# Four linear-attention and gated feed-forward layers on one core: the last segment by halves, keys of odd heads by DMA, the map of q by pairs

## The chip, the core and the metric

The kernel runs on one core of a Trainium2 chip. Its engines run side by side, each in the order of its own instructions: TensorE (PE in the profile, with its weight loads as PEld), VectorE (DVE), ScalarE (ACT), GpSimd (POOL) and SyncE (SP), which here only issues DMAs. The metric is the time of one execution on the device in microseconds; the median of several runs counts.

## The reference

The input x has 2048 rows of 512. Four blocks follow one another, each on a layer norm and added to x: attention, feed-forward, attention, feed-forward, both attention blocks with the same weights and both feed-forward blocks too.

```python
for s in range(4):                                    # segments of 512 rows; 32 heads of 16
    logits = einsum('bhqd,bhkd->bhqk', qs, ks) * scale + causal_mask
    a_dot  = einsum('bhqk,bhkd->bhqd', softmax(logits), vs)
    pq     = phi(qs)                                  # phi(t) = t + 1 where t > 0, else exp(t)
    a_mem  = einsum('bhld,bhde->bhle', pq, M) / (einsum('bhld,bhd->bhl', pq, z)[..., None] + 1e-6)
    out_s  = g * a_mem + (1 - g) * a_dot              # g = sigmoid(beta) of each head
    M, z   = M + phi(ks)^T vs, z + sum(phi(ks))
x = x + concat(out) @ wo
x = x + (gelu(norm(x) @ w_gate) * (norm(x) @ w_up)) @ w_down     # inner width 1792
```

## The kernel before

The work is cut into eight passes k = 0 to 7: segments 0 to 3 of the first pair of blocks, then of the second. A pass has an attention part (class `Att`) and a feed-forward part (class `Ffn`). All weights and x stay in SBUF. Passes overlap: while the feed-forward products of one pass run, TensorE also does the scores of the next and the q, k and v of one after that.

The order of all instructions is made in Python before anything is built. `Clocks` and `Engine` keep a book of when each engine would be free, with a cost for each kind of instruction. Work for TensorE that needs a PSUM bank is an `Item` with a due time (`DUE`, `DUE_STEP`, `BIAS`, in passes) and a condition; the main loop (L1150) takes score steps as they become possible, else the ready item that is due first, else a half score step, else a product of ones that only fills (L1181). `Engine.post` puts work on the other engines with a slack: the lower it is, the sooner the work is taken. SP takes DMAs in the order that the book gives, and an engine waits in order: what stands behind a waiting instruction waits too.

Dense work goes through `product` (L406): four matmuls of 128 rows by 32 columns of weights, one in each column group, with up to 512 moving columns. Gate, up, down, q, k, v, wo, the update of M and the memory term all use it, so they share line 411. Scores (L805) use row groups instead, so that the array changes its tiling between a score step and dense work.

In a pass, `scores` does 20 steps, five for each two blocks of four even and four odd heads (a block b is 128 of the 512 columns of q). A step fills two PSUM tiles st of 128x1024, one for each pair of heads, which ACT's exponential (L834) turns into pt; GpSimd's affine_select (L825) then zeroes what lies above the diagonal. A step may be issued in two halves, one st tile at a time. `flush_item` multiplies pt by the values (L853), for the even and then the odd heads of a block; DVE transposes (byq, L865), takes the reciprocal of the row sums (L869), scales (ab, L873), transposes back (aT, L880) and adds the memory term amT (L883). When aT has its four blocks, `wo` adds to x (L920), `Norm` takes row statistics (L434, L442) and GpSimd the inverse deviation rs (L452), DVE scales rows to xn (L464), and xn is turned into xnT by a DMA transpose (`turn_later`, L376) or, for the feed-forward norms of passes 0, 1 and 7, by products with an identity matrix. Then come 14 gate products of four steps each with the gelu on ACT (L943), 14 up products with a multiplication on DVE (L990), and for each of four row tiles a down product of 14 steps.

In a group of 32 rows the even head's keys are the first 16, which the scores read alone from kf; for the odd heads they read all 32 rows of a copy kB in which the even head's rows are zero: `k_done` makes it for each block by a multiplication with maskB (L562), on DVE in pass 0 and on GpSimd later. `phi` makes the feature map of one block of q or k: ACT's exp into one of three e tiles (L619), DVE's min with 1 (L637), and max(x, 0) + e (L623); that of k is then turned by a DMA transpose into phik.

The vaug tiles hold the values with a column for the denominators; DVE writes these columns and the constants of the gate in `gate_constants` and `later_constants` (L348 to L368).

Of the kernel before, what the change touches and what calls it, by code (L numbers as in the profile page):

```python
# [19 lines left out]
H = 32  # L20
# [15 lines left out]
PAIRS = 5  # L36
STEPS = 4 * PAIRS
# [3 lines left out]
SETS = 3  # L41
HALF_FROM = 0
# [4 lines left out]
QK_DUE = 0.628  # L47
E_Q = -0.224
E_K = 0.898

FLUSH_WAIT = 3.455
PIECE_SLACK = 1.942
URGENT, SOON, NORMAL = -5.367, -1.509, 0.0
EXP_SLACK, E_SLACK, PHI_SLACK, GELU_SLACK = -0.824, 4.309, 2.973, 1.704
ACT_EVICT, FIRST_EVICT = 1.257, 1.549
XN_BUFS = 3
KB_DVE = 1
KB_SLACK = 4.7
HALF_STEPS = 1
MARGIN = 1.0  # L60
MEM_SLACK = 0.593


DUE = {"wo": 0.876, "gate": 1.264, "up": 1.3, "down": 1.912, "upd": 0.119, "mem": 0.057, "v": -0.028}
DUE_STEP = {"gate": 0.0055, "up": 0.02, "down": 0.0585}
BIAS = {
    **{("qk", k): d for k, d in {2: 0.223, 3: 0.042, 4: 0.068, 5: 0.154, 6: 0.166, 7: 0.076}.items()},
    **{("mem", k): d for k, d in {1: -0.292, 4: -0.311, 5: 0.04, 6: -0.044, 7: -0.105}.items()},
    **{("down", k): d for k, d in {0: 0.059, 1: -0.073, 4: -0.059, 5: 0.029, 6: 0.023, 7: -0.054}.items()},
    **{("upd", k): d for k, d in {0: -0.005, 1: 0.321, 2: -0.019, 3: 0.19}.items()},  # L70
    **{("v", k): d for k, d in {0: 0.085, 2: -0.091, 3: -0.008, 4: -0.177, 5: -0.177, 6: 0.177}.items()},
    **{("wo", k): d for k, d in {1: 0.024, 2: -0.93, 3: -0.666, 4: 0.027, 5: -0.086, 7: -0.094}.items()},
    **{("gate", k): d for k, d in {1: -0.2, 3: -0.043, 4: -0.093, 5: 0.014}.items()},
    **{("up", k): d for k, d in {0: 0.121, 2: -0.039, 4: -0.056, 5: -0.013, 6: 0.024}.items()},
}

# [52 lines left out]
class Clocks:  # L129
# [4 lines left out]
    SWITCH = 0.097  # L134
# [56 lines left out]
    def has(self, *names, by=None):  # L191
        t = self.pe if by is None else by
        return all(self.ev.get(n, 1e9) <= t for n in names)


class Slots:


    def __init__(self, ck, n):
        self.ck, self.free, self.queue = ck, list(range(n)), []  # L200

    def take(self, fn):
        self.queue.append(fn)
        self.turn()

    def turn(self):
        while self.free and self.queue:
            self.queue.pop(0)(self.free.pop(0))
# [28 lines left out]
def kernel(  # L237
# [52 lines left out]
    pieces = [(14.0, 512, lambda: load_x(2)), (27.0, 512, lambda: load_x(3))]  # L290
    for kt in range(KT):
        pieces.append((32.0 + 1.2 * kt, 128, lambda kt=kt: load(w_att["o"][:, kt, :], w_view(A_wo)[:, kt, :])))
    for n, (sb, w) in enumerate(((wg_sb, B_w_gate), (wu_sb, B_w_up))):
        for kt in range(KT):
            for h in range(2):
                c = slice(FF * h // 2, FF * (h + 1) // 2)
                pieces.append((37.0 + 1.6 * (8 * n + 2 * kt + h), 224, lambda sb=sb, w=w, kt=kt, c=c: load(
                    sb[:, kt, c], w_view(w)[:, kt, c])))
    for h in range(7):
        r = slice(2 * h, 2 * h + 2)  # L300
        pieces.append((94.0 + 2.0 * h, 256, lambda r=r: load(
            wd_sb[:, r, :], B_w_down.rearrange("(ft p) n -> p ft n", p=P)[:, r, :])))

# [37 lines left out]
    zacc = cst.tile([P, 4], F32, name="zacc")  # L341
    vaugs = [cst.tile([P, TPS, VW + 15], BF16, name=f"vaug{i}") for i in range(SETS)]

# [4 lines left out]
    def gate_constants():  # L348
        nc.vector.tensor_scalar(out=cden[:], in0=tmp_e[:], scalar1=1.0, scalar2=None, op0=ALU.add)
        nc.vector.tensor_scalar(out=tmp_e2[:], in0=tmp_e2[:], scalar1=1.0, scalar2=None, op0=ALU.add)  # L350
        nc.vector.reciprocal(out=tmp_e2[:], in_=tmp_e2[:])


    def later_constants():
        def column(va):
            nc.vector.tensor_copy(out=by_head(va)[:, :, :, DH], in_=cden[:].unsqueeze(1).to_broadcast([P, TPS, H]))
            nc.vector.memset(va[:, :, VW:], 0.0)
# [7 lines left out]
        for n, va in enumerate(vaugs):  # L365
            ck.dve.post(13.0 + 3.0 * n, NORMAL, (0.4, lambda va=va: column(va), None))
        for b in range(4):
            ck.dve.post(20.0 + b, NORMAL, (0.28, lambda b=b: scale(b), None))  # L368
# [50 lines left out]
    xn_slots = Slots(ck, XN_BUFS)  # L419

    class Norm:
        def __init__(self, key, tt0, tag, slack, free):
            self.key, self.tt0, self.tag, self.slack, self.free = key, tt0, tag, slack, free
            self.mv, self.n, self.left = None, 0, TPS
# [4 lines left out]
        def stats(self, j, ready):  # L429
# [6 lines left out]
            def told(t):  # L436
                self.n += 1
                if self.n == TPS:
                    self.scales(t)
# [4 lines left out]
        def scales(self, ready):  # L444
            def first():
                self.ve = wrk.tile([P, TPS, 1], F32, tag="lnve", name="ve")
                nc.gpsimd.tensor_scalar(out=self.ve[:], in0=self.mv[:, :, 1:2], scalar1=EPS_LN, scalar2=None,
                                        op0=ALU.add)

            def second():  # L450
                self.rs = self.small("rs", 1)
                nc.gpsimd.tensor_tensor(out=self.rs[:], in0=self.ve[:], in1=mhalf[:], op=ALU.pow)  # L452

            ck.pool.post(ready, URGENT, (0.25, first, None),
                         (1.05, second, lambda t: ck.when(self.free, lambda: self.start(max(t, ck.pe)))))

        def start(self, ready):
            self.xnT = seg.tile([P, KT, L], BF16, tag=self.tag, bufs=1, name="xnT")
            for j in range(TPS):
                xn_slots.take(lambda i, j=j: self.row(j, i, max(ready, ck.pe)))  # L460
# [7 lines left out]
        def row(self, j, i, ready):  # L468
            xn = Box(lambda: self.normed(j, i))

            def landed(t):
                xn_slots.back(i, t)
                self.left -= 1
                if not self.left:
                    ev[self.key] = t

            def told(t):
                if self.key in BY_PE:
                    items.append(self.turn_item(j, xn, t, landed))
# [4 lines left out]
            ck.dve.post(ready, self.slack, (0.46, xn, told))  # L484
# [25 lines left out]
    items = []  # L510
    e_jobs = []
    e_slots = Slots(ck, 3)
# [3 lines left out]
    class Att:  # L516
        def __init__(self, k):
# [3 lines left out]
            self.ab, self.aT, self.amT, self.n_qkv, self.n_am, self.n_num = {}, None, {}, 0, 0, 0  # L521
# [7 lines left out]
        def add_items(self):  # L529
# [5 lines left out]
            def first():  # L535
                self.q, self.kf, self.kB = (seg.tile([P, KT, L], BF16, tag=f"{n}{k % SETS}", bufs=1, name=n)
                                            for n in ("q", "kf", "kB"))
# [11 lines left out]
            def q_done(b, ps):  # L549
                def told(t):  # L550
                    ev["q", k, b] = t
                    if s > 0:
                        e_jobs.append((k - E_Q + 0.03 * b, t, lambda: k < 2 or ("memn", k - (1 if s > 1 else 2)) in ev,
                                       lambda r, sl: self.phi(b, "q", r, sl)))

                evict(ps, lambda: self.q[:, b, :], lambda: ps()[:], told)

            def k_done(b, ps, at=None):
                def told(t):
                    ev["k", k, b] = t  # L560
                    eng, job, cost = (nc.vector, ck.dve, 0.345) if k < KB_DVE else (nc.gpsimd, ck.pool, 1.566)
                    job.post(t, KB_SLACK if k else NORMAL, (cost, lambda: eng.tensor_scalar(  # L562
# [654 lines left out]
```

## Time and profile before

| | us |
|---|---|
| median of 3 runs (lowest to highest) | 558.88 (557.92 to 559.39) |
| the profiled execution | 559.25 |
| its span, first to last instruction | 557.5 |
| first score step, last score step | 12.2, 496.5 |
| score exponentials on ACT (320) | 309.9 |
| masks on POOL (448) | 202.6 |
| granted clock of TensorE | 1.000 |

The span is what the trace covers; the rest of the profiled execution lies around it. Many numbers of the profile are busy times of an engine; busy on TensorE includes matmuls that run one over another, so how often products start says more than how long each took. A line such as "PE L411 MATMUL m<-xnT,wg_sb 128*32 128x512 bf16" names the engine, the line of the code, the operation, what is written and read, the shape of the weights and the moving columns.

### The profile page before, as it was taken

The page shows a single profiled execution, that of the slowest core. Times are in us where ns is not written, and L with a number is a line of the kernel's source. Part 1 is how long each engine was busy: PE and PEld are TensorE (multiplying, and loading weights), DVE is VectorE, ACT ScalarE, POOL GpSimd, SP SyncE. Part 2 cuts the span into 40 slices and gives each one's busy share as a digit, 9 for nine tenths or more (in the row PEclk, how much of TensorE's full clock was granted, in tenths as well). Part 3 has the DMA queues.
Part 4 walks back from the last instruction along what each step waited for, and adds up shares of the span by engine and source line. Part 5 has one row for each costly group of instructions (what it writes and reads, how often), then busy time and mean ns, then how long its engine had stood idle before and what let it go on. Part 6 is the DMA issues. An engine that isn't in the chain of part 4 may idle for free.

```text
span 557.5 us, 24388 instructions
## 1 busy us (share of the span) xinstructions
PE 547.4 (98%) x10882; PEld 255.0 (46%) x10882; DVE 436.5 (78%) x838; ACT 446.8 (80%) x553; POOL 270.4 (48%) x520
## 2 busy tenths in 40 slices
PE   8999999999999999999999999999989999999997
PEld 3333445444544444444444445444444444445554
DVE  5987996999969996788948899689856897577061
ACT  3999999987999789997898979989788877860600
POOL 2688973365814465274725656148522764130000
PEclk9999999999999999999999999999999999999999
DMA  7236611510041033110310033100530005000001
GB/s 226 43 95 219 125 21 32 144 42 2 16 75 31 4 40 68 21 31 4 60 21 12 3 57 56 37 12 5 96 50 3 2 9 101 12 2 31 12 2 40
DMA packets 64361, 25.96 MB, mean 47 GB/s; under 512 B 54272, under 2 KB 64256, under 8 KB 64256
## 3 DMA queue, kind: packets, MB, share of 16 engines
q1 hardware_dynamic: 64112, 24.40, 20.6%
q8 instruction: 85, 1.39, 1.0%
q14 instruction: 20, 0.16, 0.1%
q10 hardware_dynamic: 144, 0.01, 0.0%
HBM read 9.71 MB, written 2.10 MB: 21 GB/s over the span
## 4 chain that ended last, share of the span: by engine, by line
PE 83%; DVE 10%; ACT 2%; DMA 1%; issue 1%; POOL 1%; SPq 0%; ACTq 0%
PE m L411 68%; PE st L805 9%; PE m L853 6%; ACT pt L834 1%; DVE x_sb L920 1%; DVE byq L865 1%; DVE xn L464 1%; DVE e L623 1%; DVE gel L990 1%; ACT gel L943 1%; DMA phik<-e 1%; DVE e L637 1%; DVE phiq L623 1%; DMA x_sb<-in_A_x_dram 1%; DVE aT L880 1%
## 5 line engine op out<-in xcount | busy, mean ns | idle before, releaser
L834 ACT ACTIVATE pt<-st 128x1024 bf16<-128x1024 f32 x320 | 309.9, 1027 | 48.7 <-PE st L805 44.3
L825 POOL TENSOR_SCALAR_AFFINE_SELECT pt<-pt 128x256 bf16<-128x256 bf16 (+1 forms) x448 | 202.6, 471 | 218.0 <-ACT pt L834 212.4
L990 DVE TENSOR_TENSOR gel<-gel,m 128x512 bf16<-128x512 bf16 x112 | 75.3, 684 | 44.2 <-PE m L411 34.8
L411 PE MATMUL m<-xnT,wg_sb 128*32 128x512 bf16 x1792 | 106.6, 380 | 0.7 <-ACT xnT L403 0.7
L411 PE MATMUL m<-wd_sb,gel 128*32 128x512 bf16 x1792 | 106.8, 380 | 0.1
L411 PE MATMUL m<-xnT,wu_sb 128*32 128x512 bf16 x1792 | 105.8, 380 | 0.1
L411 PEld LDWEIGHTS <-wu_sb 128*32 128x32 bf16 x1792 | 46.5, 97 | 45.5 <-issue 5.7
L411 PEld LDWEIGHTS <-wg_sb 128*32 128x32 bf16 x1792 | 46.0, 97 | 44.8 <-issue 7.4
L411 PEld LDWEIGHTS <-gel 128*32 128x32 bf16 x1792 | 45.5, 97 | 45.3 <-issue 7.2
L920 DVE TENSOR_TENSOR x_sb<-x_sb,m 128x512 bf16<-128x512 bf16 x64 | 42.3, 673 | 17.4 <-PE m L411 17.4
L865 DVE STREAM_TRANSPOSE byq<-m 128x512 f32<-128x512 f32 x64 | 45.3, 707 | 12.6 <-PE m L853 12.6
L853 PE MATMUL m<-pt,vaug 128*32 128x512 bf16 (+3 forms) x1024 | 46.2, 300 | 0.6 <-DVE gel L990 0.5
L562 POOL TENSOR_SCALAR kB<-kf,maskB 128x512 bf16<-128x512 bf16 x28 | 45.0, 1608 | 1.8 <-DVE kf L402 1.1
L805 PE MATMUL st<-q,kB 32*128 32x384 bf16 (+3 forms) x512 | 39.6, 300 | 1.3 <-ACT pt L834 1.3
L434 DVE BATCH_NORM_STATS2 st<-x_sb 128x6 f32<-128x512 bf16 x60 | 40.5, 675 | 0.1
L805 PE MATMUL st<-q,kf 16*128 16x384 bf16 (+3 forms) x512 | 40.1, 302 | 0.1
L943 ACT ACTIVATE gel<-m 128x512 bf16<-128x512 f32 x63 | 34.8, 602 | 3.7 <-PE m L411 3.5
L853 PEld LDWEIGHTS <-vaug 128*32 128x32 bf16 x1024 | 26.0, 97 | 23.0 <-issue 2.1
L411 PE MATMUL m<-xnT,wk_sb 128*32 128x512 bf16 x496 | 35.4, 381 | 0.0
L411 PE MATMUL m<-xnT,wq_sb 128*32 128x512 bf16 x496 | 34.0, 380 | 0.0
L411 PE MATMUL m<-wv_sb,xnT 128*32 128x512 bf16 x512 | 33.9, 380 | 0.0
L805 PEld LDWEIGHTS <-kf 16*128 16x128 bf16 x512 | 11.9, 91 | 43.7 <-issue 42.2
(92 smaller groups left out, 568.5 us busy)
## 6 DMA issues: line engine op xcount, KB each, us to landing
out_dram<-x_sb SPq DMA_DIRECT2D x16, 128.0 KB, 1.8
wg_sb<-in_B_w_gate_dram SPq DMA_DIRECT2D x8, 224.0 KB, 4.4
wu_sb<-in_B_w_up_dram SPq DMA_DIRECT2D x8, 224.0 KB, 4.6
wd_sb<-in_B_w_down_dram SPq DMA_DIRECT2D x7, 256.0 KB, 4.2
x_sb<-in_A_x_dram SPq DMA_DIRECT2D x3, 512.0 KB, 6.7
xnT<-xn SPq DMA_TRANSPOSE x48, 2.5
x_sb<-in_A_x_dram SPq DMA_DIRECT2D x4, 128.0 KB, 3.1
wv_sb<-in_A_wv_dram SPq DMA_DIRECT2D x1, 512.0 KB, 7.6
```

Source lines behind the costliest of these rows:

```text
L411: nc.tensor.matmul(out[r], lhsT=lhsT[:, r], rhs=rhs, start=start, stop=stop, tile_position=(0, 32 * c))
L434: nc.vector.bn_stats(out=self.st6[:, 0, :], in_=x_sb[:, self.tt0 + j, :])
L562: job.post(t, KB_SLACK if k else NORMAL, (cost, lambda: eng.tensor_scalar(out=self.kB[:, b, :], in0=self.kf[:, b, :], scalar1=maskB[:, 0:1 ...
L623: nc.vector.scalar_tensor_tensor(out=dst, in0=src, scalar=0.0, in1=e[0][:], op0=ALU.max, op1=ALU.add, accum_out=self.zk[:, b:b + 1] if whi ...
L805: nc.tensor.matmul(sts[j // 2][:, j % 2, c0:c0 + N], lhsT=lhsT[rows, b, P * ki:P * ki + P], rhs=self.q[rows, b, P * ki:L], start=True, sto ...
L825: nc.gpsimd.affine_select(out=dv, in_=dv, pattern=[[0, w], [1, P]], compare_op=ALU.is_ge, fill=0.0, base=0, channel_multiplier=-1)
L834: ck.act.post(max(begun + 0.4, self.step_from), EXP_SLACK, (1.024, lambda st=st, pt=pt: nc.scalar.activation(out=pt[:], in_=st[:], func=AC ...
L853: nc.tensor.matmul(ps()[32 * j:32 * j + 32, P * ki:L], lhsT=self.vaug[:, ki, h * (DH + 1):h * (DH + 1) + 32], rhs=two[j // 2][:, j % 2, c0 ...
L865: nc.vector.transpose(out=self.byq[:, par, :, :].rearrange("p a c -> p (a c)"), in_=ps()[:])
L920: ck.dve.post(ck.made(), slack, (0.683, lambda: nc.vector.tensor_tensor(out=xt, in0=xt, in1=ps()[:], op=ALU.add), lambda t: (ps.read(t), t ...
L943: return lambda: nc.scalar.activation(out=out(), in_=in_(), func=ACT.Gelu_apprx_tanh)
L990: ck.dve.post(ck.made(), NORMAL, (0.683, lambda: nc.vector.tensor_tensor(out=g, in0=g, in1=ps()[:], op=ALU.mult), lambda t: (ps.read(t), e ...
```

## The change

Five things are done:

1. Pass 7, the last segment, is cut into two halves of 256 rows. `steps_of` gives its 20 score steps anew: first the six that the first half of the queries needs, then 14 for the second. A flush then covers even and odd heads of a block for one half, so that there are still eight. Norm, gate, up and down run for each half; gate and up products have 256 moving columns, and two of the 14 inner tiles share a PSUM bank.
2. kB lies in three fixed tiles. Those of index 1 and 2 are set to zero by GpSimd at the start; from pass 1 on, the odd heads' rows come by four DMAs on SP, of 16 partitions and 4 KB in each, when all four blocks of the keys are there. Pass 0 still multiplies on DVE.
3. The map of q is made for two blocks at once and in the phiq tile itself, without e tiles; e has two tiles now, for k alone.
4. The vaug columns are made on GpSimd ahead of the first products, and the gate's constants on DVE from 45 us of the plan on.
5. The order is planned anew: other due times, slacks and margins (1.7 us more for the transposes of phi of k, 1.5 for kB), four xn buffers, one of them kept for feed-forward rows and for pass 1, the back-transposition of a chunk no longer waiting for amT, and gate products that start the gelu part waiting for an earlier one's hold. The book's clock is set to 12.1 us after the opening part (10.9 before). The weights' DMAs keep their times.

```diff
-FLUSH_WAIT = 3.455
-URGENT, SOON, NORMAL = -5.367, -1.509, 0.0
-EXP_SLACK, E_SLACK, PHI_SLACK, GELU_SLACK = -0.824, 4.309, 2.973, 1.704
-XN_BUFS = 3
+FLUSH_WAIT = 4.904
+URGENT, SOON, NORMAL = -11.142, -0.462, 0.0
+EXP_SLACK, E_SLACK, PHI_SLACK, GELU_SLACK = -0.745, 5.402, 3.22, 1.514
+XN_BUFS = 4
+XN_KEPT = 1
+E_BUFS = 2
+PHI_MARGIN = 1.7
+KB_MARGIN = 1.5
...
+SPLIT = {NK - 1}
+def steps_of(k):
...
+    for b in (0, 2):
+        wide = [[(c, par, 0, 0, HALF, HALF * par) for par in range(2)] for c in (b, b + 1)]
+        narrow = [(c, par, 1, P, HALF, P * (2 * (c - b) + par)) for c in (b, b + 1) for par in range(2)]
+        found += [(wide[0], []), (narrow, [(b, None, 0)]), (wide[1], [(b + 1, None, 0)])]
...
+    kBs = [cst.tile([P, KT, L], BF16, name=f"kB{i}") for i in range(SETS)]
+    for kB in kBs[1:]:
+        nc.gpsimd.memset(kB[:], 0.0)
...
+    def value_constants():
+        nc.gpsimd.tensor_scalar(out=cden[:], in0=tmp_e[:], scalar1=1.0, scalar2=None, op0=ALU.add)
+        for va in vaugs:
+            nc.gpsimd.tensor_copy(out=by_head(va)[:, :, :, DH], in_=cden[:].unsqueeze(1).to_broadcast([P, TPS, H]))
+            nc.gpsimd.memset(va[:, :, VW:], 0.0)
...
+                for g in range(4):
+                    r = slice(32 * g + 16, 32 * g + 32)
+                    ck.sp.post(t, KB_SLACK, (0.55, lambda r=r: nc.sync.dma_start(
+                        out=self.kB[r], in_=self.kf[r]), lambda t2: ck.at(t2 + 1.8, lambda: landed(t2 + 2.0))))
...
-                    eng, job, cost = (nc.vector, ck.dve, 0.345) if k < KB_DVE else (nc.gpsimd, ck.pool, 1.566)
-                    job.post(t, KB_SLACK if k else NORMAL, (cost, lambda: eng.tensor_scalar(
+                    if k == 0:
+                        ck.dve.post(t, NORMAL, (0.5, lambda: nc.vector.tensor_scalar(
...
+        def phi_q(self, half, ready, slack):
+            two = slice(2 * half, 2 * half + 2)
...
+                nc.scalar.activation(out=self.phiq[:, two, :], in_=self.q[:, two, :], func=ACT.Exp)
...
+                nc.vector.tensor_scalar(out=self.phiq[:, two, :], in0=self.phiq[:, two, :], scalar1=1.0, scalar2=None,
+                                        op0=ALU.min)
...
+                nc.vector.scalar_tensor_tensor(out=self.phiq[:, two, :], in0=self.q[:, two, :], scalar=0.0,
+                                               in1=self.phiq[:, two, :], op0=ALU.max, op1=ALU.add)
...
+            def grown(w, ps, g, h):
+                return [(Clocks.MM[512] / self.parts + 0.0012 * (self.parts - 1),
+                         lambda kt=kt, f=f, n=n: product(ps()[:, n * L // self.parts:(n + 1) * L // self.parts],
+                                                         w[:, kt, f * P:(f + 1) * P], self.norm.xnT[:, kt, cols(h)],
+                                                         kt == 0, kt == KT - 1))
+                        for n, f in enumerate(tiles(g)) for kt in range(KT)]
```

554 lines of the change are left out of this document (324 added, 230 removed).

## The prediction

> **What bounds the kernel now.** I read the page first, then busy time by stage, then the chain of waits, then the timelines of the three places where TensorE is not simply working.
>
> ```profile
> PE 547.4 (98%) x10882; PEld 255.0 (46%) x10882; DVE 436.5 (78%) x838; ACT 446.8 (80%) x553; POOL 270.4 (48%) x520
> PE 83%; DVE 10%; ACT 2%; DMA 1%; issue 1%; POOL 1%; SPq 0%; ACTq 0%
> ```
>
> TensorE carries 83% of the chain. Busy is not useful, though, so I cut the span at the places where its work changes:
>
> ```profile
> 0.00:12.20 12.20, 10.21 (x54) 4.78 (x55) 5.90 (x19) 3.70 (x7) 3.53 (x14) 1.00 0.81 249
> 12.20:66.40 54.20, 54.20 (x905) 20.79 (x908) 47.63 (x103) 53.22 (x66) 43.05 (x77) 1.00 0.45 116
> 66.40:80.10 13.70, 13.57 (x328) 6.41 (x328) 13.07 (x30) 13.58 (x18) 10.83 (x19) 1.00 0.34 60
> 80.10:125.00 44.90, 43.03 (x936) 20.85 (x932) 37.91 (x72) 41.78 (x55) 21.57 (x38) 1.00 0.28 67
> 125.00:404.00 279.00, 278.73 (x5724) 128.76 (x5716) 235.18 (x454) 245.10 (x299) 147.53 (x287) 1.00 0.18 32
> 404.00:409.00 5.00, 3.29 (x108) 1.83 (x100) 2.05 (x5) 2.49 (x5) 1.79 (x4) 1.00 0.61 88
> 409.00:496.60 87.60, 87.60 (x1765) 40.49 (x1762) 66.56 (x114) 74.02 (x88) 39.28 (x78) 1.00 0.13 24
> 496.60:554.30 57.70, 56.81 (x1104) 31.04 (x1096) 27.59 (x49) 12.94 (x20) 2.79 (x6) 1.00 0.06 19
> ```
>
> The columns are window, length, then busy us of PE, weight loads, DVE, ACT, POOL, the clock and the DMA share. From 12 to 80 us ACT is full (53.22 of 54.20, 13.58 of 13.70); TensorE is "busy" but pads:
>
> ```profile
> L411 PE MATMUL m<-warm 128*32 128x512 bf16 x44 | 3.5, 383 | 0.0
> 63.53 2.56 PE L411 MATMUL m<-wo_sb,aT 128*32 128x512 bf16 x44
> 66.02 0.39 PE L805 MATMUL st<-q,kB 32*128 32x512 bf16 x4
> 66.34 0.40 PE L411 MATMUL m<-wo_sb,aT 128*32 128x512 bf16 x4
> 517.78 36.47 PE m L411 x672
> 12.20:66.40 54.20, 14.62 (x152) 4.05 (x152) 1.00 0.45 116
> 125.00:404.00 279.00, 38.62 (x584) 11.00 (x584) 1.00 0.18 32
> ```
>
> The last dense stretch prices a product (four matmuls): 36.47/672 x 4 = 0.217 us; the 44 filler matmuls are 11 products, 2.4 us. A score stretch costs its own 0.32 (66.02 to 66.34) plus 0.10 that the dense stretch before it runs over (44 x 0.0543 = 2.39, but 2.49 from start to start): 0.42. A step done in two halves pays that twice. The two windows of score matmuls alone hold 152 and 584; at 6.4 a step that is 24 and 91 steps, which the PE timeline shows in 37 and 96 stretches; 66 to 80 us has 8 for 5, 80 to 125 us 14 for 13. So 16 extra stretches before 80.1 (6.7 us), one to 125, five after (2.1 us).
>
> **The change, stage by stage.**
>
> *Before the first gate product (12.2 to 80.1).* Padding here is 6.7 + 2.4 = 9.1 us. It exists because dense work is missing until the first feed-forward block may start, 13.7 us after its last wo product (66.34; the first gate product is at 80.09):
>
> ```profile
> 66.47 2.94 ACT pt L834 x3
> 69.47 1.78 POOL pt L825 x4
> 71.70 1.51 POOL rs L452
> 73.23 1.22 DVE xn L464 x3
> 76.11 0.69 DVE xnT L402
> 78.65 0.68 DVE xnT L402
> L562 POOL TENSOR_SCALAR kB<-kf,maskB 128x512 bf16<-128x512 bf16 x28 | 45.0, 1608 | 1.8 <-DVE kf L402 1.1 <-ACT kf L403 0.6
> L619 ACT ACTIVATE e<-q 128x512 bf16<-128x512 bf16 x24 | 15.4, 644 | 1.1 <-DVE ab L873 1.1
> L943 ACT ACTIVATE gel<-gel 128x1024 bf16<-128x1024 bf16 x21 | 22.4, 1068 | 0.0
> L623 DVE SCALAR_TENSOR_TENSOR phiq<-q,e 128x512 bf16<-128x512 bf16 x24 | 18.0, 749 | 0.8
> ```
>
> These are rs, xn and its turn, waiting their turn behind masks, feature maps and evictions. The change takes 28 x 1.608 = 45 us off POOL; makes the exponentials of q 12 x 1.068 = 12.8 instead of 15.4 us of ACT; makes the adds 12 pieces between 0.749 (all fixed) and 1.498 us (none fixed), so 9 to 18 against 18.0 us of DVE (I take 15.5); moves the vaug columns from DVE to POOL; and keeps one xn buffer for feed-forward rows with more urgency. None of these engines ends the chain for long, so their savings count only here. The rows of the chain itself sum to 8.8 us of the 13.7; some 5 are queueing. I take 4 us of the 9.1; bounds 0 (exponentials still fill ACT) and 9.1.
>
> *80.1 to 125.* Idle 44.90 - 43.03 = 1.9 plus one stretch, 2.3 in all, where TensorE waits on masks, gelus and the chunk transposes. Lighter DVE and POOL should take half: -1.2, bounds 0 and -2.3.
>
> *125 to 496.6.* There TensorE has 279.00 - 278.73 = 0.3 idle, five stretches (2.1) and one stall of 5.00 - 3.29 = 1.7, while a transpose lands:
>
> ```profile
> 402.22 3.93 DMA phik<-e
> DMA to landing us min/median/max: 2.4/2.5/4.6
> ```
>
> It landed 1.4 us beyond its median. The new plan books 1.7 us more for these transposes (PHI_MARGIN), about what was lost. -1.7 of 4.1, bounds 0 and -4.1. What is late next if the transpose slips again is the update of M, then the mem products; dense work stands ahead of them in the new order.
>
> *The tail.* After the last score at 496.6 all is dense. Only 57.70 - 56.81 = 0.9 is idle, mostly the turn of the last feed-forward rows:
>
> ```profile
> 517.13 0.61 ACT xnT L403
> 499.80 0.54 PE m L853 x16
> L411 PEld LDWEIGHTS <-wg_sb 128*32 128x32 bf16 x1792 | 46.0, 97 | 44.8 <-issue 7.4
> 75.79 1.16 PE L411 MATMUL m<-vaug,phik 128*32 128x128 bf16 x64
> 76.78 0.81 PE L411 MATMUL m<-xnT,wq_sb 128*32 128x512 bf16 x12
> ```
>
> With two halves, the second half's flush, wo, norm and turn stand beside the first half's 84 products (84 x 0.217 = 18 us): -0.8, bounds 0 and -0.9. The work itself does not shrink: 20 score steps, the same columns in flushes, gate, up and down. So the split by itself is worth little in a tail that is already dense; this is where I differ from the change's headline. The halved gate and up products (896 matmuls of 256 columns for 448 of 512) cost from nothing (a flush of 512, 384, 256 and 128 columns takes 0.54 for 1280 columns at the dense rate, 512 per 0.217) to 1.9 us: 64 matmuls of 128 columns take 0.99 from 75.79 to 76.78, 2 ns each over that rate, x 896. I take +0.3, nearer the flush, which has 256 columns in it. The eight smaller chunks cost DVE at most a second set of reciprocal, scaling, back-transposition and addition, four times 2.2 = 8.9 us by the chain's 0.35 + 0.71 + 0.70 + 0.45; hidden by DVE's 30 idle us after 496.6 (57.70 - 27.59); without that cover they would be 8.9 us. A second change of ACT's table for the second half hides in ACT's 45 idle us there.
>
> Here a rule speaks against the change. The Trainium skill (TensorE: Matmul & The Clock Gate, section The mechanism) says that a weight load overlaps running matmuls only where the row group differs; column tiles share it, so each added load would be exposed. By its section on LDWEIGHTS, 32 columns take some 27 ns, so 448 added loads would make an estimated 12 us. This trace disagrees: products of 512 columns with four loads go at 0.217 us, which leaves no room for exposed ones.
>
> *The start.* Two memsets of 128x2048 join POOL ahead of the first rs.
>
> ```profile
> 0.82 0.20 POOL L323 MEMSET ident<- 128x128 bf16 x1
> 0.78 0.10 POOL L321 MEMSET mhalf<- 128x4 f32 x1 [0.29 <-POOLq L1201]
> 5.68 0.23 POOL L1041 TENSOR_SCALAR ve<-mv 128x2 f32<-128x2 f32 x1 [3.32 <-DVE mv L1038]
> ```
>
> From 4 to 128 elements costs 0.1 us more, so 2048 cost some 1.7 and two 3.5 us, in 3.32 of idle: +0.2, bounds 0 and +3.5 were they not hidden. The planner's later first instant (12.1 for 10.9) only meets where this trace stands (12.2) and is no cost.
>
> *Keys by DMA.* 28 copies of 64 KB join SP, four per segment, issued once all four key blocks are evicted; nearest rows:
>
> ```profile
> out_dram<-x_sb SPq DMA_DIRECT2D x16, 128.0 KB, 1.8
> x_sb<-in_A_x_dram SPq DMA_DIRECT2D x4, 128.0 KB, 3.1
> 0.79 1.83 SPq L274 DMA_DIRECT2D x_sb<-in_A_x_dram  x4
> ```
>
> Issue is 0.46 each, landing 1.8 to 3.1, so 3.6 to 4.9 us from the last eviction to the last landing; the plan books about 5.7. On SP they stand among the transposes of xn, phi of k and am: a copy that waits for its keys holds these, and they hold the next segment's q, k and v, the update of M and the memory term. On TensorE the third score step of a segment waits for them, with every product behind it. If the plan holds: 0.
>
> Sum: -4 -1.2 -1.7 -0.8 +0.3 +0.2 = **-7.2**. The profiled execution took 559.25 (span 557.5 and 1.75 around it), giving 552.05; the median shown is 0.37 lower, so **551.7**. Bounds of the terms: -16.4 and +5.4, 542.5 to 564.3.
>
> **Rivals.** *The padding goes almost whole* (18%): the first gate comes as its own chain allows, term one is -8 and the rest near its bounds: -13, 546. For: POOL and DVE both carry queues in front of that chain. Against: exponentials keep ACT full there.
>
> *ACT keeps the head* (15%): ACT's 53.22 of 54.20 is exponentials and nothing before segment 1 has a q map to save; the head gives nothing and one stall is gone: -1.7 -0.8 +0.5 = -2, 556.9; with the stall appearing elsewhere, 558.6, no change (7% of the 15).
>
> *Keys come late* (14%): copies queue behind transposes (landing up to 4.6) and TensorE stands at the third step of seven segments. Stalls of 1.0 us a segment eat the 7.2: that is the point from which it decides. If a landing slips as the worst transpose did, 4.6 for 2.5, 0.8 of the 2.1 is booked (5.7 for 4.9) and 1.3 stays: 7 x 1.3 = 9.1, +1.9 in all, 561. Against: most keys are made well before their segment.
>
> *Loads exposed at 256 columns* (3%): 448 x 26 ns (46.0/1792) = 11.5, 563. The Trainium skill's rule above is this rival; the flush row speaks against it.
>
> **How the numbers follow.** The forecast, 548.5 to 555.5 by its own terms, has 50%; with 546 and 556.9 (18 and 8%), faster holds 0.76. No change within 0.3% (1.7 us, about what a measurement of this kernel can tell) holds 0.07, slower 0.17. The range, 544 to 561.5, takes in the late keys' 561 and the whole padding's 546, and leaves out exposed loads and the far ends of the bounds.
>
> **What would show it.** Right: fewer than 6 extra score stretches and few fillers before the first gate, that gate at 74 to 77 us; no stall of over 1 us on phik; no idle between the last turn and the dense tail; a tail at 0.217 a product, 0.108 for halves; kB copies landed before the third step. Wrong: waits of TensorE on kB, a gate at 80, or a first score later than 12.5.

## The result, and the profile after

| | before | after |
|---|---|---|
| median of 4 runs each on the same chip, us | 558.73 (557.92 to 559.39) | 553.99 (553.54 to 554.37) |
| profiled execution / its span, us | 559.25 / 557.5 | 553.54 / 551.8 |
| first score, first gate product, us | 12.20, 80.09 | 12.37, 79.98 |
| last score matmul, us | 496.5 | 497.1 |

The ratio of the medians is 0.9915, with an interval of 0.9903 to 0.9927: 4.74 us less, where 7.2 less were forecast (551.7; its range, 544 to 561.5, held the result). The profiled execution before lies 0.5 us above its kernel's median and the one after 0.5 below, so the two traces differ by 5.7 us, 1 us more than the medians. Three summary rows of the changed kernel's page, in the order of those of before:

```profile
PE 545.1 (99%) x11478; PEld 267.0 (48%) x11478; DVE 429.9 (78%) x814; ACT 449.9 (82%) x550; POOL 233.4 (42%) x471
PE 93%; ACT 3%; DVE 1%; DMA 1%; POOL 1%; issue 0%; ACTq 0%
L456 PE MATMUL m<-warm 128*32 128x512 bf16 x64 | 5.1, 383 | 0.0
```

TensorE carries 93% of the chain (83% before). POOL is 37 us lighter, but the filler matmuls grew from 44 to 64, so 11 fill products became 16. The same cuts of the span as in the prediction (window, length, busy us of PE, weight loads, DVE, ACT, POOL, clock, DMA share):

```profile
12.40:68.80 56.40, 56.40 (x953) 21.82 (x956) 49.25 (x101) 55.23 (x68) 33.74 (x72) 1.00 0.55 130
68.80:80.00 11.20, 11.20 (x277) 5.53 (x273) 10.56 (x23) 11.20 (x16) 7.68 (x15) 1.00 0.61 118
80.00:125.00 45.00, 44.92 (x952) 21.41 (x944) 36.60 (x66) 42.85 (x54) 17.32 (x35) 1.00 0.31 50
404.00:409.00 5.00, 5.00 (x165) 2.83 (x157) 4.90 (x10) 4.72 (x7) 2.93 (x6) 1.00 0.44 44
497.30:548.30 51.00, 50.96 (x1452) 38.64 (x1448) 23.26 (x42) 13.16 (x20) 3.11 (x6) 1.00 0.07 22
```

From 12 to 80 us ACT is as full as it was (55.23 of 56.40, 11.20 of 11.20) and the first gate product is no earlier. From 80 to 125 us TensorE's idle time fell from 1.87 to 0.08 us. The stall on the transposes of phi of k between 404 and 409 us is gone (5.00 busy of 5.00, 3.29 before). After the last score 51.0 us of dense work are left instead of 57.7, without a gap.

To see the rest, I took every matmul of the trace, from its start to the start of the next, and subtracted what its columns cost at the dense pace of the prediction (0.217 us for 512 columns on the whole array, a quarter of it on a quarter); fillers count as nothing useful. What is left is time that TensorE was not usefully at work: idle, padding, and the price of changing between score and dense work. Us per stage, from the first matmul at 1.1 us on:

| stage of the span, us | before | after | difference | predicted |
|---|---|---|---|---|
| to the first score | 8.49 | 8.66 | +0.2 | +0.2 |
| first score to 80 | 16.22 | 16.79 | +0.6 | -4 |
| 80 to 140 | 7.82 | 5.28 | -2.5 | -1.2 (to 125) |
| 140 to 436 | 27.87 | 24.71 | -3.2 | with the last, |
| 436 to the end | 6.13 | 5.13 | -1.0 | -1.7 -0.8 +0.3 |
| sum | 66.5 | 60.6 | -6.0 | -7.2 |

The -6.0 is what TensorE's last matmul gained, which ends at 548.3 instead of 554.2 us; what follows it took 0.2 us longer, so the span fell by 5.7. A second trace of the changed kernel (experiment 11) sums to 61.6, 4.9 less than before: its opening is 0.7 us longer, and its other stages differ from those of the first trace by up to 0.3 us, so a single stage shouldn't be read closer than that. Two rows of a view by stage show most of the 140 to 436 line, first before, then after:

```profile
140.00:436.00 296.00, 294.02 (x6076) 136.75 (x6076) 241.54 (x458) 260.31 (x319) 147.66 (x289) 1.00 0.19 33
```

```profile
140.00:436.00 296.00, 295.43 (x6132) 138.30 (x6132) 241.30 (x448) 263.35 (x320) 132.03 (x278) 1.00 0.24 38
```

Idle fell from 1.98 to 0.57 us, and the score matmuls stand in 95 stretches there instead of 98: 1.4 and, at 0.42 a stretch, 1.3 of the 3.2 us. One of the three stretches has only moved across the cut at 140 us: from 80 to 436 us there are 115 instead of 117. The rest of the 3.2 wasn't told apart. So the gain lies behind the head, in stages from which the prediction took 3.4 of its 7.2 us; the head, from which it took most, gave none.

**The head.** TensorE's timeline of the changed kernel (start, us, engine, line, what, count):

```profile
60.56 0.73 PE L956 MATMUL m<-pt,vaug 128*32 128x512 bf16 x16
...
63.94 1.03 PE L456 MATMUL m<-wo_sb,aT 128*32 128x512 bf16 x16
...
68.39 0.60 PE L456 MATMUL m<-wo_sb,aT 128*32 128x512 bf16 x8
...
79.98 0.84 PE L456 MATMUL m<-xnT,wg_sb 128*32 128x512 bf16 x12
```

From the last wo product (68.6) to the gate takes 11.4 us, where it took 13.7: the chain of rs, xn and its turn did become 2.3 us shorter. But the wo products themselves come 2.2 us later (68.6 for 66.4). Both together are nothing.

The chain didn't become shorter by the keys or the paired maps: with either of them undone and the order kept (experiments 2, 3 and 12), it takes 11.4 us as well. One difference that the rows do show is the fourth xn. Before, it comes 2.3 us after the first three have ended (73.23 and 1.22 in the prediction's chain), behind the eviction of xnT at 76.11 that gives one of the three buffers back; after, with four buffers, all four follow one another. First before, then after:

```profile
76.71 0.41 DVE L464 TENSOR_SCALAR xn<-x_sb,mv,rs 128x512 bf16<-128x512 bf16 x1
```

```profile
74.98 1.95 DVE L515 TENSOR_SCALAR xn<-x_sb,mv,rs 128x512 bf16<-128x512 bf16 x4
```

No run changes the number of buffers alone, so how much of the 2.3 us they make is not shown.

**Halves.** The first and the second half's gate products, and the turn that separates them:

```profile
511.05 6.29 PE L456 MATMUL m<-xnT,wg_sb 128*32 128x256 bf16 x224
517.16 0.62 PE L456 MATMUL m<-ident,xn 128*32 128x128 bf16 x32
...
518.52 6.30 PE L456 MATMUL m<-xnT,wg_sb 128*32 128x256 bf16 x224
```

224 matmuls in 511.05 to 517.16 are 56 products in 6.11 us, 0.109 each: half of 0.217. The added weight loads cost nothing, and the rule of the Trainium skill weighed in the prediction (TensorE: Matmul & The Clock Gate, The mechanism) doesn't hold for column tiles here. (The same section of the Trainium skill names a background weight buffer beside the row groups, which the prediction left out; no run here shows it.)

**Keys and maps.** A DMA row, the landing line of its queue, and the two groups of the paired map of q:

```profile
kB<-kf SPq DMA_DIRECT2D x28, 64.0 KB, 2.9
DMA to landing us min/median/max: 2.3/2.9/4.5
L692 ACT ACTIVATE phiq<-q 128x1024 bf16<-128x1024 bf16 x12 | 12.8, 1069 | 0.0
L699 DVE SCALAR_TENSOR_TENSOR phiq<-q,phiq 128x1024 bf16<-128x1024 bf16 x12 | 15.1, 1259 | 0.4
```

The landings of kB are within the prediction's 1.8 to 3.1 by the median, and no wait of TensorE is on kB. The exponentials take the 12.8 us and the adds 15.1 of the 15.5 that were estimated.

### The profile page after: what moved, and what is told of

Same layout as the page of the kernel before. It is cut to its first block, busy times and chain, and to the rows that moved or that the text cites. A ratio compares the mean times of both kernels' runs of the same rounds, so it can differ in the third digit from the quotient of the medians.

```text
span 551.8 us, 25523 instructions
## 1 busy us (share of the span) xinstructions
PE 545.1 (99%) x11478; PEld 267.0 (48%) x11478; DVE 429.9 (78%) x814; ACT 449.9 (82%) x550; POOL 233.4 (42%) x471
## 4 chain that ended last, share of the span: by engine, by line
PE 93%; ACT 3%; DVE 1%; DMA 1%; POOL 1%; issue 0%; ACTq 0%
PE m L456 76%; PE st L893 10%; PE m L956 7%; ACT pt L924 2%; ACT gel L1105 1%; DMA x_sb<-in_A_x_dram 1%; DVE xn L515 1%; DVE st L1189 0%; POOL rs L502 0%; DVE x_sb L1053 0%; ACT L1105 0%; POOL pt L911 0%; PE m L555 0%; PE m L858 0%; PE m L853 0%
## 5 line engine op out<-in xcount | busy, mean ns | idle before, releaser
L911 POOL TENSOR_SCALAR_AFFINE_SELECT pt<-pt 128x512 bf16<-128x512 bf16 (+2 forms) x416 | 203.4, 505 | 264.1 <-ACT pt L924 258.0
L456 PE MATMUL m<-xnT,wg_sb 128*32 128x512 bf16 (+1 forms) x2016 | 106.1, 356 | 0.0
L456 PE MATMUL m<-xnT,wu_sb 128*32 128x512 bf16 (+1 forms) x2016 | 105.6, 356 | 0.1
L456 PEld LDWEIGHTS <-wu_sb 128*32 128x32 bf16 x2016 | 52.4, 97 | 39.7 <-issue 4.8
L456 PEld LDWEIGHTS <-wg_sb 128*32 128x32 bf16 x2016 | 51.4, 97 | 37.6 <-issue 4.2
L956 PE MATMUL m<-pt,vaug 128*32 128x256 bf16 (+3 forms) x1088 | 46.5, 293 | 0.0
L893 PE MATMUL st<-q,kB 32*128 32x256 bf16 (+3 forms) x544 | 39.7, 291 | 0.4 <-ACT pt L924 0.4
L893 PE MATMUL st<-q,kf 16*128 16x256 bf16 (+3 forms) x544 | 39.7, 294 | 0.1
L956 PEld LDWEIGHTS <-vaug 128*32 128x32 bf16 x1088 | 24.0, 96 | 21.3 <-issue 7.0
L515 DVE TENSOR_SCALAR xn<-x_sb,mv,rs 128x512 bf16<-128x512 bf16 x64 | 30.6, 523 | 2.5 <-POOL rs L502 1.9
```

What stands on the lines that cost most here:

```text
L456: nc.tensor.matmul(out[r], lhsT=lhsT[:, r], rhs=rhs, start=start, stop=stop, tile_position=(0, 32 * c))
L515: nc.vector.tensor_scalar(out=xn[:], in0=x_sb[:, self.tt0 + j, :], scalar1=self.mv[:, j, 0:1], scalar2=self.rs[:, j, :], op0=ALU.subtract, ...
L893: nc.tensor.matmul(sts[j // 2][:, j % 2, c0:c0 + q1 - q0], lhsT=lhsT[rows, b, P * ki:P * ki + P], rhs=self.q[rows, b, q0:q1], start=True, ...
L911: nc.gpsimd.affine_select(out=dv, in_=dv, pattern=[[0, w], [1, P]], compare_op=ALU.is_ge, fill=0.0, base=0, channel_multiplier=-1)
L956: nc.tensor.matmul(ps()[32 * j:32 * j + 32, q0 + shift:q1 + shift], lhsT=self.vaug[:, ki, h * (DH + 1):h * (DH + 1) + 32], rhs=step["pt"][ ...
```

## The experiments

Medians, with the ratio to the kernel before on the same chip. "Loss" is the time without useful work worked out as above; "the changed kernel" is the one after. Where a kernel has an order planned anew, only the planner's numbers (dues, slacks, waits) differ, found by a search over the planner's own account of time; the diff shows one or two of some eighty, and an added number overrides the one that stands above it.

**1. No split, nothing else.** The planner runs with the other numbers unchanged.

```diff
-SPLIT = {NK - 1}
+SPLIT = set()
```

> Only the split of the last segment is undone; all other numbers are those of the changed kernel, and TensorE's order is the same up to the last passes. Theory A (the split only closes the idle at the end of the tail, 0.9 us, and a re-planned order did the rest): 554.6 to 555.6 us, with the wait before the last pass's first gate product back in the trace and the score steps of the last pass ending about where they did (497). Rival B (the split is what moved 6 us of dense work ahead of the last score): 557 or more.

563.02 us (562.22 to 563.42), 1.0066 [1.0048, 1.0084]: slower than both kernels. The time is in rival B's range, and the wait is the one that theory A named, 5.9 us instead of 0.9. TensorE's order is the changed kernel's until some 436 us, and loss to there is the same within 0.2 us; all of the 9 us is behind it (13.65 for 5.13). Its timeline and two windows:

```profile
508.23 3.63 PE L456 MATMUL m<-wo_sb,aT 128*32 128x512 bf16 x64
517.06 1.90 PE L456 MATMUL m<-ident,xn 128*32 128x128 bf16 x64 [5.21 <-DVE xn L515]
519.66 2.72 PE L456 MATMUL m<-xnT,wg_sb 128*32 128x512 bf16 x30 [0.70 <-ACT xnT L448]
```

```profile
496.40:556.90 60.50, 54.59 (x1036) 28.43 (x1028) 25.59 (x44) 13.26 (x20) 2.87 (x7) 0.94 0.05 17
511.00:520.00 9.00, 3.09 (x84) 2.08 (x80) 6.09 (x14) 2.05 (x4) 1.27 (x2) 0.70 0.01 2
```

After the last wo product TensorE has nothing left and stands 5.21 us for the last norm and 0.70 for its turn, and the granted clock falls to 0.70 in that stretch and 0.94 over the tail. Between 511 and 522 us the loss is 7.8 of the 8.5: 5.9 of idle and 1.9 of products that go slower, the granted clock being 0.50 from 516 to 520 us. Five fill products, at 442 and 494 us, add 1.1, of which 0.4 comes back elsewhere. So in *this* order the second half is what stands beside the last norm. It doesn't say what halves are worth in general, which is why experiment 8 exists.

**2. Odd heads' keys by POOL again, same order.** The plan still books the DMAs, so that TensorE's instructions keep their order; the multiplication is issued at each eviction.

```diff
-                    ck.sp.post(t, KB_SLACK, (0.55, lambda r=r: nc.sync.dma_start(
-                        out=self.kB[r], in_=self.kf[r]), lambda t2: ck.at(t2 + 1.8, lambda: landed(t2 + 2.0))))
+                    ck.sp.post(t, KB_SLACK, (0.55, None,
+                        lambda t2: ck.at(t2 + 1.8, lambda: landed(t2 + 2.0))))
...
-                    else:
-                        odd_heads(t)
+                    else: odd_heads(t); nc.gpsimd.tensor_scalar(out=self.kB[:, b, :], in0=self.kf[:, b, :],
+                        scalar1=maskB[:, 0:1], scalar2=None, op0=ALU.mult)
```

> The odd heads' keys of passes 1 to 7 are multiplied on GpSimd, one block at each eviction, in place of the 28 DMAs; the order on TensorE and ScalarE is that of the changed kernel instruction by instruction. Theory A (GpSimd had room, its relief is worth nothing by itself): 553.7 to 554.7, POOL busy 233 + 44 = 277 us. Rival C (masks were held by the multiplications, and their relief carries the gain): 556 or more, with exponentials or flushes that wait for masks.

555.30 us (555.17 to 556.17), 0.9937 [0.9914, 0.9960], between the ranges of theory A and rival C. POOL's timeline, then TensorE's:

```profile
46.73 1.56 POOL L641 TENSOR_SCALAR kB<-kf,maskB 128x512 bf16<-128x512 bf16 x1 [0.72 <-DVE tmp_e L402]
48.24 2.20 POOL L911 TENSOR_SCALAR_AFFINE_SELECT pt<-pt 128x256 bf16<-128x256 bf16 x6
```

```profile
48.08 1.21 PE L956 MATMUL m<-pt,vaug 128*32 128x512 bf16 x16
...
65.39 1.04 PE L456 MATMUL m<-wo_sb,aT 128*32 128x512 bf16 x16
```

A flush that took 0.73 us takes 1.21 because its masks stand behind a key multiplication, and the wo products start 1.45 us later than after, of which 0.68 came from the opening. Matmul by matmul against the changed kernel, 0.78 us arise at three flushes between 33 and 50 us and none over the 480 us that follow, although POOL works 276.5 us instead of 233.4. That is the DMAs' worth in this order: POOL's 43 us count only in the head. What order could be planned without them, no run shows.

**3 and 12. Map of q by single blocks, same order**, in two separate jobs:

```diff
-nc.scalar.activation(out=self.phiq[:, two, :], in_=self.q[:, two, :], func=ACT.Exp)
+for b in (2 * half, 2 * half + 1): nc.scalar.activation(out=self.phiq[:, b, :], in_=self.q[:, b, :], func=ACT.Exp)
```

The clamp and the add are cut the same way.

> Each of the 12 paired maps of q is issued as two instructions of one block on ScalarE and two each on VectorE; TensorE's order is unchanged. Theory A: ScalarE gets 2.6 us more in all and VectorE 5, both off the path: 553.8 to 554.6. Rival C (relief of ScalarE and VectorE carries the gain): 556 or more.

> The single-block maps of q again, beside the changed kernel. If they cost nothing, as the traces say (both run the same order and stand 0.6 us apart from the first 15 us on, without more by 520 us), the two medians lie within 0.5 us of each other; if the pairs are worth 0.8 us, this one is 0.6 to 1.0 us above.

554.80 (554.49 to 554.94) and 554.22 us (553.89 to 554.52); the changed kernel in the second job, **experiment 11**:

> The changed kernel unaltered, on the same chip as the next one, to tell what a difference of 0.8 us between two of these runs means. All theories: 553.5 to 555.

554.70 us (553.62 to 555.04). The pairs are worth nothing that can be measured: side by side the single blocks are 0.5 us faster, within the spread, and stage by stage experiment 12's trace has the losses of the changed kernel's first trace within 0.04 us. Experiment 3's trace stands 0.6 us behind that one from the opening on, and this begins in one row: after, then experiment 3.

```profile
1.11 5.86 PE L359 MATMUL m<-warm 128*128 128x512 bf16 x19 [1.11 <-DVE warm L350]
```

```profile
1.11 7.02 PE L359 MATMUL m<-warm 128*128 128x512 bf16 x19 [1.11 <-DVE warm L350]
```

The same 19 matmuls; from the first score to 520 us the two traces keep their distance. Behind 520 us experiment 3 has two stops of 0.3 us among the halved up products, and experiment 11 has one such stop among the gate products; what causes them is open. Experiment 11 has this late start too (first score at 13.06), so it is the better one to compare the next kernels' stages with: its losses are 9.35, 16.74, 5.10, 24.96 and 5.44 us.

**4. All parts of the change with the old numbers** (dues, slacks, three xn buffers, none kept, three e tiles, no margin for phi of k):

```diff
-FLUSH_WAIT = 4.904
+FLUSH_WAIT = 3.455
...
-XN_BUFS = 4
-XN_KEPT = 1
+XN_BUFS = 3
+XN_KEPT = 0
...
-PHI_MARGIN = 1.7
+PHI_MARGIN = 0.0
```

> All parts of the change stay, but due times, slacks, buffers and margins are those of the kernel before, so the order is planned with the old numbers. Theory A (the numbers carry the gain): 556.5 to 560. Rival B or C (the parts carry it): 555 or less.

576.95 us (575.6 to 578.2), 1.0315 [1.0278, 1.0353], far above what either side expected. The parts with numbers not made for them lose 18 us to the kernel before, so this run says neither that the numbers carry the gain nor that the parts do. Its largest wait on TensorE (total, times, longest):

```profile
PE m L456 <- DMA phik<-e: 4.3, 2, 3.2
```

**5 and 6. One number back at a time.**

```diff
-FLUSH_WAIT = 4.904
+FLUSH_WAIT = 3.455
```

> One number of the plan goes back: a flush waits 3.455 us for a score step before it is taken as dense work, as in the kernel before, not 4.904. Theory A (the later flush is why the first wo product came 1.7 us later than before and ate what the shorter norm chain won): the first gate product comes at 78 to 79 us in place of 80.0. Rival D (ScalarE's exponentials alone set that instant): it stays at 79.5 to 80.5. For the whole time theory A expects 555 to 563, worse than the changed kernel, since all later numbers were fitted to another order; 553 or less would say that numbers can be moved singly.

566.72 us (566.22 to 567.22), 1.0139 [1.0118, 1.0159]. Its TensorE timeline:

```profile
63.10 2.13 PE L456 MATMUL m<-wo_sb,aT 128*32 128x512 bf16 x36
...
77.97 2.34 PE L456 MATMUL m<-xnT,wg_sb 128*32 128x512 bf16 x40
```

With the old wait the gate is at 78.0 instead of 80.0, as theory A had it. So FLUSH_WAIT, the time for which the planner puts a flush off while score steps are left (4.9 us instead of 3.5), is what held the gate at 80: with it the first segment's last flush, and wo behind it, come 0.8 to 1.8 us later. But the loss to 80 us is the same (16.7 for 16.8), and the kernel is 13 us slower, beyond the 563 that was allowed: loss from 140 to 436 us is 34.7 for 24.7, and one number has moved every later choice of the planner. Part of the 10 us is the clock, which fell twice in that stage; the first time (window, length, busy us of PE, weight loads, DVE, ACT, POOL, clock, DMA share):

```profile
142.00:145.40 3.40, 2.38 (x32) 0.66 (x28) 3.30 (x9) 3.40 (x5) 3.05 (x6) 1.00 0.20 39
145.50:148.80 3.30, 3.30 (x48) 1.14 (x40) 3.27 (x9) 3.18 (x5) 2.60 (x5) 0.50 0.40 80
```

It is 0.50 again from 210.4 to 213.7 us. Two stretches of 3.4 us at half the clock make an estimated 3.4 us.

```diff
-PHI_MARGIN = 1.7
+PHI_MARGIN = 0.0
```

> The plan books 1.7 us less for the transposes of phi of k; nothing else changes but what the planner makes of it. Theory A (the margin keeps TensorE from standing at the update of M): one or more waits of TensorE on phik, 1 to 4 us in all, and a time of 555 to 563. Rival: no wait on phik, and a time within 1 us of 554.

564.97 us, a single run, 2 us above theory A's range. The wait on phi of k returns, 1.2 us once, as theory A had it, and the order around it is another one: loss from 140 to 436 is 31.0. Neither of the two says what its number is worth, only that the numbers can't be moved one by one.

**7. The margin in the kernel before**, where the order hardly moves:

```diff
-turn_later(t, NORMAL, lambda: self.phik[:, :, b * P:(b + 1) * P], lambda: e[0][:], there)
+turn_later(t, NORMAL, lambda: self.phik[:, :, b * P:(b + 1) * P], lambda: e[0][:], there, 1.7)
```

> The kernel before with that margin of 1.7 us alone. Theory A: the wait of 1.7 us on phik at 404 us is gone, and the time is 557 to 561, the numbers being those of another order. Rival E (one stall is all that can be had by margins): 557.0 to 557.5, 1.7 us less than before and nothing else moved.

557.98 us (557.39 to 559.28) against 559.07, 0.9984 [0.9972, 0.9997], in theory A's range; the span is 555.8 for 557.5. The wait, 1.7 us before, is now

```profile
PE m L411 <- DMA phik<-e: 0.2, 1, 0.2
```

Loss from 140 to 436 is 26.2 for 27.9. The term of 1.7 us for this stall was right, and it is half of what that stage gained.

**8. No split, order planned anew for it.**

```diff
+FLUSH_WAIT = 5.086
...
-SPLIT = {NK - 1}
+SPLIT = set()
```

> All parts of the change but the split; the plan's numbers are sought anew for this kernel, from a start as poor as that of the run with the split. Theory A' (after the run without the split: the split frees the last pass's cover, so that dense work can be used up earlier; the rest of the gain needs it): 556 to 558, with TensorE idle for 0.5 us or more between the last wo product and the last gate products, or more down products of pass 6 left after the last score step. Rival F (any order that is fitted to this kernel does as well): 553.5 to 555.

556.35 us (555.73 to 556.68), 0.9951 [0.9937, 0.9965]: 6.7 us of experiment 1's loss come back without any halves, and the time is in the range of theory A'. Its TensorE timeline after the last score:

```profile
498.01 3.19 PE L474 MATMUL m<-wd_sb,gel 128*32 128x512 bf16 x56
501.03 3.63 PE L474 MATMUL m<-wo_sb,aT 128*32 128x512 bf16 x64
504.49 6.22 PE L474 MATMUL m<-wd_sb,gel 128*32 128x512 bf16 x112
510.53 0.84 PE L474 MATMUL m<-ident,xn 128*32 128x128 bf16 x48
511.63 0.41 PE L474 MATMUL m<-ident,xn 128*32 128x128 bf16 x16 [0.25 <-ACT xnT L466]
511.95 3.21 PE L474 MATMUL m<-wd_sb,gel 128*32 128x512 bf16 x56
514.97 12.27 PE L474 MATMUL m<-xnT,wg_sb 128*32 128x512 bf16 x224
```

As theory A' had it, down products of pass 6 are kept back and laid beside the last norm, 112 and 56 matmuls of them; the longest gap is 0.25 us. Its losses are 9.32, 17.08, 7.22, 24.70 and 5.40 us: beside experiment 11's the tail is equal (5.40 and 5.44), and the 2.1 us by which the spans differ (1.7 by the medians) lie between 80 and 140 us (7.22 and 5.10), where this order has four more score stretches (23 for 19, 1.7 us) and three fill products (0.6). Whether that is the price of keeping dense work back, or only a search that ended early, is open.

**9. The kernel before with an order planned anew** (with the margin of 1.7 and the later clock, none of the other parts):

```diff
+FLUSH_WAIT = 2.577
...
-ck.pe, ck.act.free, ck.dve.free, ck.pool.free, ck.sp.free = 10.9, 11.5, 11.5, 10.0, 9.0
+ck.pe, ck.act.free, ck.dve.free, ck.pool.free, ck.sp.free = 12.1, 12.7, 12.8, 11.2, 9.0
```

> None of the parts of the change: the kernel before with its book's clock set to the trace (12.1 us), the margin of 1.7 us for phi of k, and numbers sought anew in the same way. Theory A': 557 to 559.5, so the parts are needed for the order that the change has. Rival F: 554 to 556.

561.24 us (559.25 to 564.42 in 12 runs), 1.0040 [1.0022, 1.0058]. A miss for both sides: this search found nothing better than the old order, and a wait on phi of k of 2.7 us stands in it again. In the profiled execution, the slowest of the twelve, the clock falls behind that wait; the fastest six take 559.25 to 560.40, no less than the kernel before. It doesn't show that no better order exists.

**10. The changed kernel, order sought anew from FLUSH_WAIT 3.455**, to keep the gate at 78 without the 13 us:

```diff
-FLUSH_WAIT = 4.904
+FLUSH_WAIT = 3.455
...
+FLUSH_WAIT = 2.55
...
```

> The changed kernel with numbers sought anew from a flush wait of 3.455 us, in the same way as for the two others. Theory A': 552.5 to 554, as good as the changed kernel or 1 us better, since with the split an order of this kind is found again from elsewhere; dense work of pass 6 and of the first half covers the last norm. Rival F: within 1 us of the run without the split. If it is under 553.5 it beats both kernels.

554.52 us (553.85 to 556.17), 0.9924 [0.9908, 0.9939], 0.5 us above theory A' and 1.8 below the run without the split, so not as rival F had it either. The gate is at 78.1, and nothing is gained: the loss to 80 us falls by 0.3 beside experiment 11's (16.44 for 16.74), that from 140 to 436 rises by 0.8 (its profiled execution, at 556.17, is its slowest). An earlier gate is not a shorter kernel by itself. No version beat the changed kernel by more than the spread; experiment 12's 554.22 lies between its two medians, 553.99 and 554.70.

## Why the prediction was right, and where it was not

**Right: the direction and what bounds the kernel; the size partly by luck.** TensorE stayed the bound. Its loss fell by 6.0 of the 7.2 us in the first trace, by 4.9 in the second, and the medians by 4.7. That the sum came so near is in part luck: the head missed by 4.6 us in one direction (+0.6 for -4), the stages from 80 us on by 3.3 us in the other (-6.7 for -3.4).

**The head, -4, was the step that failed.** It came out at +0.6. The term was built on the chain from wo to gate: "some 5 are queueing. I take 4 us". That chain did become 2.3 us shorter, though not by the keys or the maps of q, which leave it at 11.4 us when they are undone. But the step took the start of the chain as fixed. The longer FLUSH_WAIT moved the wo products back by 2.2 us, and experiments 5 and 10 show the gate at 78 with a shorter wait; experiment 10 shows besides that the gate's time was the wrong measure. The head's padding (45 score stretches to 80 us in both kernels, 16 fill products for 11) is dense work that is missing, and an earlier gate took as much from later stages as it gave. By the prediction's own signs the head is a miss: it wanted fewer than 6 extra score stretches, where there are 16 as before, and the gate at 74 to 77 us, and had named a gate at 80 as a sign of being wrong. The rival that ACT keeps the head was right on what this stage gave and wrong on the rest. Its reason agrees with the trace (ACT 11.20 of 11.20 us before the gate), but no run takes load off ACT there, and experiment 5 shows that ACT alone doesn't hold the gate at 80.

**Relief of POOL and DVE counts only in the head: confirmed for the keys**, and smaller than taken. Experiment 2 puts the 45 us off POOL at 0.78 us, all of it between 33 and 50 us; experiments 3, 11 and 12 put the pairs of q at nothing.

**80 to 125, -1.2, was mis-sized**: 1.8 us of idle went instead of half of 1.9, and by the loss 2.8 us in all (6.65 to 3.88), beyond the bound of 2.3; to 140 us, 2.5.

**125 to 496.6, -1.7, was mis-sized.** The stall went as stated, worth 1.7 us of span by experiment 7. The step left out that an order planned anew may also save score stretches and other waits in the middle: from 140 to 436 alone 3.2 us went. The bound of 4.1 held.

**The tail, -0.8 and +0.3**: -0.8 behind the last score (1.06 to 0.25), 0.5 in experiment 11's trace. The halves' price is 0 by the 0.109 us a product, so the flush row was the right one to lean on and the rival of exposed loads falls. "The split by itself is worth little in a tail that is already dense" is borne out by experiment 8, whose tail is as dense without it; experiment 1 adds what the prediction didn't see, that within the new order the split can't be taken away, since that order spends the dense work of pass 6 early. But the whole kernel of experiment 8 is 1.7 to 2.4 us slower than the changed one, and whether that is the split is open.

**Start, +0.2**: +0.2 in the first trace, but +0.9 in experiment 11's, whose first score at 13.06 is beyond the prediction's 12.5; that the first came out as forecast is luck. The two memsets took 3.55 us of POOL, as worked out, and the first xn comes no later for them (7.04 for 7.10). The +0.2 comes from a part that the prediction booked as relief alone: the vaug columns, which GpSimd now writes while VectorE makes the fourth xn (last section).

**Late keys** did not happen: landings of up to 4.5 us, as the rival had it, but no wait.

What stays open: by 7, 2 and 3 with 12, the margin (1.1 by the medians, 1.7 by the spans), the keys (0.8) and the pairs (0) make 2 to 2.5 of the 4.7 us, if they may be added up, which no run shows. The rest belongs to the order, with the xn buffers, the vaug columns and the split that it was planned for; they weren't told apart.

## What to carry to other kernels

Read where the loss of the bounding engine lies, stage by stage, before and after, matmul by matmul: a chain that gets shorter in the profile (here 13.7 to 11.4 us) is worth nothing if its start moves as well. In a kernel whose order comes from a planner, parts and numbers are one thing: experiments that put one number back cost 11 to 13 us and price neither, while those that hold the order fixed and change what an instruction does price a part to a few tenths. Cutting the last stage into halves is one way to have dense work beside its norm; keeping earlier work back for it is another, and the tail came out as dense, though that kernel as a whole was slower by 1.7 us for a reason that stays open.

## What the runs showed of the hardware

The same opening block of 19 matmuls took 5.86 us in one execution and 7.02 in another, 5.93 and 6.96 in experiments 12 and 11. In the traces of the changed kernel and its variants the first score comes at 12.4 to 12.6 us where the block ended by 7.8 us, and at 13.0 to 13.1 where it ended at 8.0 or later, while an order that is the same keeps its times from there to 520 us. Single profiles of two kernels shouldn't be compared closer than that without looking at this row.

Stands shorter than the 5.2 us of experiment 1 lower the granted clock too. After one of 2.7 us in experiment 9 it was 0.50 for some 3.4 us (window, length, busy us of PE, weight loads, DVE, ACT, POOL, clock, DMA share):

```profile
406.00:408.40 2.40, 0.10 (x8) 0.00 (x0) 0.71 (x2) 1.38 (x2) 1.53 (x4) 1.00 0.35 90
408.50:411.80 3.30, 2.97 (x72) 1.83 (x76) 1.34 (x4) 0.75 (x1) 0.00 (x0) 0.50 0.20 40
411.90:416.00 4.10, 4.10 (x96) 1.93 (x88) 3.12 (x6) 3.62 (x6) 2.26 (x4) 1.00 0.17 36
```

After the 1.7 us of the kernel before it stayed at 1.00. In experiment 5 it fell with no single stand above 0.7 us, after a stretch in which TensorE was busy for 2.38 of 3.40 us. The changed kernel's traces show no fall while products run.

VectorE was slowed beside GpSimd: the fourth xn of the opening takes 0.40 us before, and 0.63 after, where GpSimd now writes the vaug columns at that time. In order: before; after, with two rows of GpSimd; experiment 11:

```profile
9.25 0.40 DVE L464 TENSOR_SCALAR xn<-x_sb,mv,rs 128x512 bf16<-128x512 bf16 x1
```

```profile
9.19 0.63 DVE L515 TENSOR_SCALAR xn<-x_sb,mv,rs 128x512 bf16<-128x512 bf16 x1
8.89 0.73 POOL L397 COPY vaug<-cden 128x128 bf16<-128x128 bf16 x1
9.48 0.93 POOL L397 COPY vaug<-cden 128x128 bf16<-128x128 bf16 x1
```

```profile
9.61 0.90 DVE L515 TENSOR_SCALAR xn<-x_sb,mv,rs 128x512 bf16<-128x512 bf16 x1
```

It is so in every trace: 0.40 us in the three kernels that have GpSimd idle at that time (before, experiments 7 and 9), 0.62 to 0.98 in the eleven others. That agrees with the Trainium skill (SBUF — State Buffer, Who interferes with whom), by which VectorE and GpSimd share a pair of SBUF ports.
